# Column halves of w_out and 512-token MoE1 tiles in the first chunk of a windowed-attention and gated-MLP kernel

## The chip, the core and the metric

The kernel runs on one core of a Trainium2 chip. The metric is the time of one execution on the device in microseconds (us), lower is better. TensorE (PE) multiplies matrices into PSUM, which has eight banks of 128 partitions by 512 fp32 values here. ScalarE (ACT), VectorE (DVE), GpSimd (POOL) and SyncE (SP) are the other engines; POOL and SP here mainly issue DMAs.

## The reference

Attention over a causal window of 128 positions with a linear position bias, for 8 batches of 8 heads, 576 positions and head size 64; then a gated MLP on the 4608 resulting tokens of width 512.

```python
scores = scale * np.matmul(q, k.transpose(0, 1, 3, 2))
bias = slopes[:, None, None] * (-np.abs(rel).astype(np.float32))[None, :, :]
mask = (rel >= 0) & (rel < window)
scores = np.where(mask, scores + bias[None], -1000000000.0)
attn = np.exp(scores - np.max(scores, axis=-1, keepdims=True))
attn = attn / (np.sum(attn, axis=-1, keepdims=True) + 1e-09)
x = np.matmul(attn, v)          # (8, 8, 576, 64)
x = x.transpose(0, 2, 1, 3).reshape(4608, 512)
h = x @ w_in                    # w_in 512 x 2048
g = h * np.cos(h)
out = g @ w_out                 # w_out 2048 x 512
```

## The kernel before

**Stages.** The 4608 tokens are cut into nine chunks of 512. For each chunk, MoE1 computes h transposed: a feature block of 128 rows (fc, 16 of them) by tokens, summed over four blocks kc of the width 512. ScalarE takes sin(h + pi/2) from the PSUM bank into `cos`, VectorE multiplies bank and `cos` into the bf16 tile `gT`. MoE2 then computes, for each of the four 128-token tiles t of the chunk, 128 x 512 outputs as a sum of 16 matmuls over fc in one bank; ScalarE or VectorE copies the bank to `ob`, and SP stores it. MoE1 of later chunks (`moe1`) has matmuls of 512 tokens. MoE1 of chunk 0 (`moe1_block`) works by single tiles: a block is four features by 128 tokens in one bank, so it can start when one tile of x is there. There are 16 such blocks, in the hand-written list `order`, with banks in rotation from `seq`.

**Attention.** A unit (b, qb, hh) is one block of 128 queries of a batch and half of the heads, or all heads at the two ends (qb 0 and qb 4, the last of 64 queries). Its steps are scores on PE (`scores`), exp on ScalarE (`exps`), a multiplication by exp(bias) and mask on VectorE (`mask`), the product with v on PE (`pv`), a normalisation (`norm`), and a transpose into xT, on PE with a copy out of PSUM (`x_pe`) or by a DMA of SP (`x_dma`). Units in `BIASED` have the bias added on PE instead, as two matmuls of 512 columns with the identity ahead of their scores, and `mask` returns at once for them. Seven units of batch 0 come before chunk 0; the units for the next chunk's tokens are worked between MoE1 and MoE2 of each chunk. q and k of batches 0 and 1 are transposed on PE (`qk_transposes`, four banks and four copies for batch 1 and each of q and k); later batches' by DMAs of SP from `qnat` and `knat`.

**Banks.** `UB` = 2, 3 hold pv results, `OB` = 0, 1 the MoE2 results, `SB` = 4 to 7 scores; each is also used for other work.

**Order.** The class `Plan` takes all operations in the order in which the functions call `op`, with the buffers that each reads (`r`) and writes (`w`), an estimate of how long its engine is occupied (`occ`) and when its result is there (`lat`), and a priority `pri` (lower goes first). `schedule` lays out a fixed list for each engine from these estimates: among operations that are ready it takes the higher priority, then the earlier one. On the chip every engine runs its list in order and waits on semaphores. So a DMA that is really later than its estimate holds whatever stands behind its user in that engine's list. Attention has priorities 0 to 2, MoE1 3 to 5, MoE2 6, so that MoE2 fills the gaps of the attention. DMAs of POOL are issued in the order of the calls: `load_w_out` (line 429) issues four pieces, each of four feature blocks by all 512 columns, before `load_v(1)` and the loads of `qnat` and `knat`.

## Time and profile before

| | us |
|---|---|
| Median of three runs (309.72 to 310.37) | 310.05 |
| The profiled execution | 310.24 |
| Its span, first to last instruction | 308.4 |
| DVE busy | 195.8 |
| ACT busy | 200.3 |
| POOL busy | 97.0 |

The mean granted TensorE clock of the profiled execution was 1.000 of full speed. "Lnnn" is a line of the kernel; a row of a timeline has the start in us, the duration in us, the engine, the line, the operation, output and inputs, and how many instructions were merged; in square brackets stands the idle time of the engine before them and what ended it. Matmuls overlap: a merged row of n matmuls is longer than n times the issue interval by the length of the last one's pipeline, and some matmul records are missing, so the weight loads (PEld) count them better. The granted clock, the DMA share and GB/s stand at the end of the rows of a window.

### The profile page before, as it was taken

To read this page: it belongs to the slowest core of one execution; us is meant where nothing else is said; L and a number is where in the kernel's file an instruction comes from. 1 tells how busy PE (TensorE), PEld (TensorE's weight loads), DVE (VectorE), ACT (ScalarE), POOL (GpSimd) and SP (SyncE) were. 2 spreads that over 40 slices of the span, in tenths; PEclk is the share of its full clock that TensorE was granted. 3 is DMA by queue.
4 is the path that set the end of the run, shared out by engine and by line. 5 is a ranking of instruction groups with operands and counts; after the bars stand their busy time and mean duration, and the time that the engine had idled before them with its cause. 6 is when DMAs were issued, how large, how long until landed. Compare 5 with 4: busy or idle time off the path is not lost.

```text
span 308.4 us, 6675 instructions
## 1 busy us (share of the span) xinstructions
PE 299.5 (97%) x2685; PEld 162.1 (53%) x2726; DVE 195.8 (63%) x409; ACT 200.3 (65%) x267; POOL 97.0 (31%) x122
## 2 busy tenths in 40 slices
PE   8889999999999999999999999999999999999996
PEld 6679755445554455445544554455445554444444
DVE  7688777574668566856785568656966588742000
ACT  6887973875478745873688378746964488752211
POOL 8997200455055505550347123900500000000000
PEclk9999999999999999999999999999999999999999
DMA  9999999999499958998699969995991420001112
GB/s 147 179 204 207 206 162 193 132 183 154 122 121 138 172 98 154 133 175 98 157 114 149 167 88 180 150 184 114 143 113 44 113 70 0 0 0 70 68 71 99
DMA packets 150333, 39.09 MB, mean 127 GB/s; under 512 B 138912, under 2 KB 145312, under 8 KB 150304
## 3 DMA queue, kind: packets, MB, share of 16 engines
q0 software_dynamic: 100688, 18.10, 79.5%
q1 hardware_dynamic: 49344, 20.33, 33.3%
q8 instruction: 21, 0.34, 0.5%
q10 hardware_dynamic: 272, 0.26, 0.3%
q14 instruction: 8, 0.07, 0.1%
HBM read 36.70 MB, written 9.44 MB: 150 GB/s over the span
## 4 chain that ended last, share of the span: by engine, by line
PE 90%; DMA 3%; POOL 2%; ACT 2%; issue 1%; DVE 1%; POOLq 0%; ACTq 0%
PE ps L812 38%; PE ps L759 36%; PE ps L568 5%; PE ps L784 4%; DMA w_inb<-in_moe_w_in_dram 3%; ACT p L595 2%; PE ps L642 2%; PE ps L644 2%; PE ps L630 1%; POOL vp L391 1%; PE ps L509 1%; DVE p L614 1%; PE ps L634 1%; POOL qrows L383 0%; PE ps L721 0%
## 5 line engine op out<-in xcount | busy, mean ns | idle before, releaser
L812 PE MATMUL ps<-w_outb,gT 128*128 128x512 bf16 (+2 forms) x566 | 132.1, 373 | 2.5 <-issue 1.3
L759 PE MATMUL ps<-xT,w_inb 128*128 128x512 bf16 x499 | 113.9, 379 | 0.7
L768 DVE TENSOR_TENSOR gT<-ps,cos 128x512 bf16<-128x512 f32 x128 | 85.1, 688 | 19.6 <-ACT cos L764 14.7
L764 ACT ACTIVATE cos<-ps,halfpi 128x512 f32<-128x512 f32 x128 | 84.6, 687 | 18.0 <-PE ps L759 13.9
L812 PEld LDWEIGHTS ps<-w_outb,gT 128*128 128x128 bf16 x592 | 53.4, 98 | 55.7 <-DVE ob L820 0.3
L595 ACT ACTIVATE p<-ps 128x1024 bf16<-128x1024 f32 x64 | 61.5, 1023 | 31.2 <-PE ps L568 31.0
L759 PEld LDWEIGHTS ps<-xT,w_inb 128*128 128x128 bf16 x512 | 49.0, 98 | 56.2 <-ACT p L595 0.6
L391 POOL DMA_DIRECT2D vp<-in_v_dram x40 | 33.7, 870 | 87.6 <-DMA xT<-xnat 67.4
L614 DVE TENSOR_TENSOR p<-p,emask 128x1024 bf16<-128x1024 bf16 x59 | 39.7, 684 | 27.8 <-ACT p L595 27.8
L819 ACT ACTIVATE ob<-ps 128x512 f32<-128x512 f32 (+2 forms) x21 | 12.1, 576 | 41.6 <-PE ps L812 35.2
L402 POOL DMA_DIRECT2D qnat<-in_q_dram x30 | 25.3, 877 | 22.5 <-DMA qt<-qnat 22.5
L402 POOL DMA_DIRECT2D knat<-in_k_dram x30 | 25.4, 884 | 12.3 <-DMA kt<-knat 9.8
L820 DVE COPY ob<-ps 128x512 f32<-128x512 f32 x16 | 11.0, 685 | 15.8 <-PE ps L812 15.7
L681 DVE TENSOR_TENSOR xnat<-ps,rec 128x256 bf16<-128x256 f32 x48 | 19.9, 421 | 1.3
L568 PE MATMUL ps<-qt,kt 64*128 64x128 bf16 (+1 forms) x576 | 19.4, 211 | 0.3 <-DVE qt L525 0.2
L642 PEld LDWEIGHTS ps<-vp,p 128*128 128x128 bf16 x192 | 14.2, 97 | 9.9 <-issue 6.4
L568 PEld LDWEIGHTS ps<-qt,kt 64*128 64x128 bf16 x576 | 14.5, 94 | 8.7 <-issue 3.5
L642 PE MATMUL ps<-vp,p 128*128 128x65 bf16 x192 | 17.4, 193 | 0.7 <-DVE xT L731 0.5
L644 PE MATMUL ps<-vp,p 128*128 128x65 bf16 x192 | 17.5, 193 | 0.0
L784 PE MATMUL ps<-xT,w_inb 128*128 128x128 bf16 x256 | 16.0, 219 | 0.6 <-DMA w_inb<-in_moe_w_in_dram 0.6
L784 PEld LDWEIGHTS ps<-xT,w_inb 128*128 128x128 bf16 x256 | 14.5, 98 | 1.3 <-DMA w_inb<-in_moe_w_in_dram 0.8
L644 PEld LDWEIGHTS ps<-vp,p 128*128 128x128 bf16 x192 | 13.2, 97 | 2.2
(66 smaller groups left out, 160.9 us busy)
## 6 DMA issues: line engine op xcount, KB each, us to landing
out_dram<-ob SPq DMA_DIRECT2D x35, 256.0 KB, 2.2
vp<-in_v_dram POOLq DMA_DIRECT2D x32, 128.0 KB, 7.1
qnat<-in_q_dram POOLq DMA_DIRECT2D x24, 128.0 KB, 6.5
knat<-in_k_dram POOLq DMA_DIRECT2D x24, 128.0 KB, 5.1
w_outb<-in_moe_w_out_dram POOLq DMA_DIRECT2D x4, 512.0 KB, 21.8
w_inb<-in_moe_w_in_dram POOLq DMA_DIRECT2D x3, 512.0 KB, 12.2
qrows<-in_q_dram POOLq DMA_DIRECT2D x1, 576.0 KB, 15.5
krows<-in_k_dram POOLq DMA_DIRECT2D x1, 576.0 KB, 17.5
```

The lines of the kernel that those rows point to most:

```text
L391: op("pool", [lambda e, t=t, rows=rows: e.dma_start(vp[b % 2][0:rows, t, :, 0:64], v[b, :, 128 * t:128 * t + rows, :].rearrange("h p d -> ...
L402: fns.append(lambda e, t=t, rows=rows: e.dma_start(nat[which][0:rows, t, :, :], src[b, :, 128 * t:128 * t + rows, :].rearrange("h p d -> p ...
L568: ins = e.matmul(ps[:, banks[x], c0:c0 + n_], keys_ap(b, x, pr, kc), query_ap(b, x, pr, qb, n_), start=not acc, stop=stop)
L595: op("act", lambda e: e.activation(P[i][:, 0:1024], ps[:, banks[0]:banks[0] + 2, :].rearrange("p a b -> p (a b)"), ACTF.Exp, scale=0.125), ...
L614: op("dve", lambda e: e.tensor_tensor(p, p, m, ALU.mult), r=[("P", i), ("EM", 0), ("EM", 1)], w=[("P", i)], occ=600, lat=690, pri=1)
L642: e.matmul(o, P[i][:, c0:c0 + 128], V[:, qb - 1, h, 0:65], start=True, stop=False)
L644: ins = e.matmul(o, P[i][:, c0 + 128:c0 + 256], V[:, qb, h, 0:65], start=False, stop=True)
L759: op("pe", lambda e, kc=kc: e.matmul(ps[:, bank, :], w_in[:, kc, 128 * fc:128 * fc + 128], xT[:, kc, r0:r0 + CH], start=(kc == 0), stop=(k ...
L764: op("act", lambda e: e.activation(cosb[ci][:, :], ps[:, bank, :], ACTF.Sin, bias=halfpi[:, 0:1]), r=["halfpi"], w=[("B", bank), ("cos", c ...
L768: op("dve", lambda e: e.tensor_tensor(gT[gi][:, fc, :], ps[:, bank, :], cosb[ci][:, :], ALU.mult), r=[("cos", ci)], w=[("B", bank)] + [("g ...
L784: ins = e.matmul(ps[:, bank, 128 * i:128 * i + 128], w_in[:, kc, 128 * fc:128 * fc + 128], xT[:, kc, t0:t0 + 128], start=(kc == 0), stop=( ...
L812: op("pe", lambda e, t=t, fc=fc, bank=bank, j0=j0, j1=j1: e.matmul(ps[:, bank, 0:j1 - j0], gT[gi][:, fc, 128 * t:128 * t + 128], w_out[:, ...
```

## The change

Five things change, all in chunk 0 or ahead of it.

1. `BIASED` has one more unit, (0,3,0).
2. `load_w_out` loads w_out in quarters of eight feature blocks by 256 columns: columns 0-255 in pieces 0 and 1, columns 256-511 in pieces 2 and 3. The DMA's runs in DRAM become 1 KB instead of 2 KB, and 512 B instead of 1 KB in SBUF; the issue estimate goes from 750 to 900 ns.
3. `moe1_block` becomes `moe1_part`, which takes f1 - f0 features by t1 - t0 tiles with 512 values a partition in all: for features 0-3 single tiles as before, for features 4-7 two features by two tiles (matmuls of 256 columns), and features 8-15 go through `moe1` with 512-token matmuls. Banks come from a list.
4. The batch-1 transposes are called after the 11th and 14th of the sixteen and always use banks 2 to 5.
5. MoE2 of chunk 0 is `moe2_first`: for each half of the columns all four tiles in the order 0, 2, 1, 3, tiles 0 and 1 side by side in bank 0, tiles 2 and 3 in bank 1; a copy for each bank and a store of 256 rows by 256 columns.

```diff
@@ -336,7 +336,7 @@
         GROUPS = [[2] * 4] + [[3, 3, 2]] * 5 + [[3] * 3]
         SLOT = [4, 6, 2]
         QUOTA = [8, 8, 8, 8, 8, 8, 9]
-        BIASED = [(0, 0, 0)] + [(0, qb, hh) for qb in range(1, 3) for hh in range(2)]
+        BIASED = [(0, 0, 0)] + [(0, qb, hh) for qb in range(1, 4) for hh in range(2)][:5]
         SB, UB, OB = [4, 5, 6, 7], [2, 3], [0, 1]
 
         slopes = [2.0 ** (-8.0 * (h + 1) / H) for h in range(H)]
@@ -427,10 +427,13 @@
                lat=1300 * (f1 - f0))
 
         def load_w_out(u):
+
+            f0, j0 = 8 * (u % 2), 256 * (u // 2)
             op("pool", [lambda e: e.dma_start(
-                w_out[:, 4 * u:4 * u + 4, :],
-                moe_w_out[512 * u:512 * u + 512, :].rearrange("(f p) j -> p f j", p=128))],
-               w=[("wo", u)], dma=f"wo{u}", occ=750, lat=2600)
+                w_out[:, f0:f0 + 8, j0:j0 + 256],
+                moe_w_out[128 * f0:128 * f0 + 1024, j0:j0 + 256].rearrange(
+                    "(f p) j -> p f j", p=128))],
+               w=[("wo", u)], dma=f"wo{u}", occ=900, lat=2600)
 
         def constants():
             op("dve", lambda e: e.memset(zeros[:, :], 0.0), w=["zeros"], occ=60, pri=0)
@@ -770,32 +773,32 @@
                r=[("cos", ci)], w=[("B", bank)] + [("g", gi, fc, t) for t in range(4)], occ=606,
                lat=692, pri=3)
 
-        def moe1_block(t, f4, bank):
+        def moe1_part(f0, f1, t0, t1, bank):
 
             ci = ccount[0] % NCOS
             ccount[0] += 1
-            t0 = 128 * t
-            for i in range(4):
-                fc = 4 * f4 + i
-
-                def f(e, i=i, fc=fc):
+            n, w = f1 - f0, 128 * (t1 - t0)
+            for i in range(n):
+
+                def f(e, i=i):
                     ins = None
                     for kc in range(NPAIR):
                         ins = e.matmul(
-                            ps[:, bank, 128 * i:128 * i + 128],
-                            w_in[:, kc, 128 * fc:128 * fc + 128], xT[:, kc, t0:t0 + 128],
-                            start=(kc == 0), stop=(kc == NPAIR - 1))
+                            ps[:, bank, w * i:w * i + w],
+                            w_in[:, kc, 128 * (f0 + i):128 * (f0 + i) + 128],
+                            xT[:, kc, 128 * t0:128 * t1], start=(kc == 0), stop=(kc == NPAIR - 1))
                     return ins
-                op("pe", f, r=xkeys(range(NPAIR), t0, 128) + [("wi", fc // 2)], w=[("B", bank)],
-                   occ=232, lat=400, pri=5)
+                op("pe", f, r=xkeys(range(NPAIR), 128 * t0, w) + [("wi", (f0 + i) // 2)],
+                   w=[("B", bank)], occ=w * 427 // 256 + 18, lat=w * 427 // 256 + 186, pri=5)
             op("act", lambda e: e.activation(cosb[ci][:, :], ps[:, bank, :], ACTF.Sin,
                                              bias=halfpi[:, 0:1]),
                r=["halfpi"], w=[("B", bank), ("cos", ci)], occ=586, lat=687, table=1, pri=3)
             op("dve", lambda e: e.tensor_tensor(
-                gT[0][:, 4 * f4:4 * f4 + 4, t0:t0 + 128],
-                ps[:, bank, :].rearrange("p (i t) -> p i t", i=4),
-                cosb[ci][:, :].rearrange("p (i t) -> p i t", i=4), ALU.mult),
-               r=[("cos", ci)], w=[("B", bank)] + [("g", 0, 4 * f4 + i, t) for i in range(4)],
+                gT[0][:, f0:f1, 128 * t0:128 * t1],
+                ps[:, bank, :].rearrange("p (i t) -> p i t", i=n),
+                cosb[ci][:, :].rearrange("p (i t) -> p i t", i=n), ALU.mult),
+               r=[("cos", ci)],
+               w=[("B", bank)] + [("g", 0, fc, t) for fc in range(f0, f1) for t in range(t0, t1)],
                occ=606, lat=692, pri=3)
 
         def moe2(c):
@@ -812,7 +815,7 @@
                         op("pe", lambda e, t=t, fc=fc, bank=bank, j0=j0, j1=j1: e.matmul(
                             ps[:, bank, 0:j1 - j0], gT[gi][:, fc, 128 * t:128 * t + 128],
                             w_out[:, fc, j0:j1], start=(fc == 0), stop=(fc == NFC - 1)),
-                           r=[("g", gi, fc, t), ("wo", fc // 4)], w=[("B", bank)],
+                           r=[("g", gi, fc, t), ("wo", fc // 8), ("wo", 2 + fc // 8)], w=[("B", bank)],
                            occ=w * 427 // 1024 + 3, lat=w * 427 // 1024 + 166, pri=6)
                     o, i = ob[oi][:, 0:w], ps[:, bank, 0:w]
                     op(("act", "dve"),
@@ -824,6 +827,32 @@
                     op("sp", [lambda e, o=o, row=row, j0=j0, j1=j1: e.dma_start(
                         out[row:row + 128, j0:j1], o)],
                        r=[("ob", oi)], dma=f"st{oi}", occ=350, lat=0)
+
+        def moe2_first():
+
+            for y in range(2):
+                j0 = 256 * y
+                for t in (0, 2, 1, 3):
+                    for fc in range(NFC):
+                        op("pe", lambda e, t=t, fc=fc, j0=j0: e.matmul(
+                            ps[:, OB[t // 2], 256 * (t % 2):256 * (t % 2) + 256],
+                            gT[0][:, fc, 128 * t:128 * t + 128], w_out[:, fc, j0:j0 + 256],
+                            start=(fc == 0), stop=(fc == NFC - 1)),
+                           r=[("g", 0, fc, t), ("wo", 2 * y + fc // 8)], w=[("B", OB[t // 2])],
+                           occ=109, lat=275, pri=6)
+                for n, bank in enumerate(OB):
+                    oi = 2 * y + n
+                    o = ob[oi][:, :]
+                    i = ps[:, bank, :]
+                    op(("act", "dve"),
+                       {"act": lambda e, o=o, i=i: e.activation(o, i, ACTF.Copy),
+                        "dve": lambda e, o=o, i=i: e.tensor_copy(o, i)},
+                       w=[("B", bank), ("ob", oi)], occ={"act": 490, "dve": 606},
+                       lat={"act": 590, "dve": 691}, pri=6)
+                    o = out[256 * n:256 * n + 256, j0:j0 + 256].rearrange("(t p) j -> p t j", p=128)
+                    i = ob[oi][:, :].rearrange("p (t j) -> p t j", t=2)
+                    op("sp", [lambda e, o=o, i=i: e.dma_start(o, i)],
+                       r=[("ob", oi)], dma=f"st{oi}", occ=400, lat=0)
 
         ucount = [0]
 
@@ -910,17 +939,16 @@
         next_t, next_v = 2, 2
         for c in range(NCH):
             if c == 0:
-                seq = OB + SB[2:4] + SB[0:2]
-                order = [(0, 0), (1, 0), (2, 0), (0, 1), (1, 1), (2, 1), (3, 0), (3, 1)] + [
-                    (t, f4) for f4 in (2, 3) for t in range(4)]
-                at = 0
-                for i, (t, f4) in enumerate(order):
-                    moe1_block(t, f4, seq[at % 6])
-                    at += 1
-                    if i in (9, 12):
-                        qk_transposes(1, "q" if i == 9 else "k", 0, range(2),
-                                      UB + [seq[at % 6], seq[(at + 1) % 6]])
-                        at += 2
+                parts = [(0, 4, 0, 1), (0, 4, 1, 2), (0, 4, 2, 3), (4, 6, 0, 2), (6, 8, 0, 2),
+                         (0, 4, 3, 4), (4, 6, 2, 4), (6, 8, 2, 4)]
+                banks = [0, 1, 6, 7, 4, 5, 0, 1, 0, 1, 6, 7, 0, 1, 6, 7]
+                for i, bank in enumerate(banks):
+                    if i < len(parts):
+                        moe1_part(*parts[i], bank)
+                    else:
+                        moe1(0, i, bank)
+                    if i in (10, 13):
+                        qk_transposes(1, "q" if i == 10 else "k", 0, range(2), UB + SB[0:2])
                 load_nat("q", q, 2)
                 load_nat("k", k, 2)
             else:
@@ -941,7 +969,7 @@
                 if next_t < B:
                     load_nat("q", q, next_t)
                     load_nat("k", k, next_t)
-            moe2(c)
+            moe2_first() if c == 0 else moe2(c)
         R.schedule(filler=lambda e: e.matmul(ps[:, UB[1], 0:128], zeros[:, :],
                                              zeros[:, :], start=True, stop=True),
                    fill=(900, 8300))
```

## The prediction

> **What bounds the kernel now.** I read the page's busy times, the chain of work that ended last and the costliest groups, then the timelines of the engines around the edit, then the waits and windows of TensorE (PE) behind it.
>
> ```profile
> span 308.4 us, 6675 instructions
> PE 299.5 (97%) x2685; PEld 162.1 (53%) x2726; DVE 195.8 (63%) x409; ACT 200.3 (65%) x267; POOL 97.0 (31%) x122
> PE 90%; DMA 3%; POOL 2%; ACT 2%; issue 1%; DVE 1%; POOLq 0%; ACTq 0%
> L812 PE MATMUL ps<-w_outb,gT 128*128 128x512 bf16 (+2 forms) x566 | 132.1, 373 | 2.5 <-issue 1.3
> ```
>
> PE is busy for 97% of the span and is 90% of the chain. So a change gains only what it takes off PE's work or out of PE's waits, and loses only what it adds there. Most of a matmul's listed duration overlaps the next one; its price on PE is its share of a run of them, from the chain:
>
> ```profile
> 23.81 5.02 PE ps L784 x88
> 54.26 8.20 PE ps L759 x38
> ```
>
> The first row gives 57 ns for 128 columns (5.02/88), the second 216 ns for 512 (8.20/38). A line through both is 4 ns plus 0.414 ns a column, so I estimate 110 ns for 256 columns, a form of w_in and w_out matmul that the trace lacks.
>
> **The start, where PE still waits.** From PE's timeline:
>
> ```profile
> 17.33 0.84 PE L784 MATMUL ps<-xT,w_inb 128*128 128x128 bf16 x12 [0.63 <-DMA w_inb<-in_moe_w_in_dram]
> 18.01 0.19 PE L642 MATMUL ps<-vp,p 128*128 128x65 bf16 x1
> 19.47 0.20 PE L642 MATMUL ps<-vp,p 128*128 128x65 bf16 x1 [0.50 <-DVE xT L731]
> ```
>
> The brackets show 0.63 us until w_in's second piece lands, then 0.50 us until an eviction of x. The row at 18.01 is the pv of unit (0,3,0), the one at 19.47 that of (0,3,1). What goes before them, on ScalarE and VectorE:
>
> ```profile
> 16.74 1.02 ACT L595 ACTIVATE p<-ps 128x1024 bf16<-128x1024 f32 x1 [0.23 <-PE ps L568]
> ```
> ```profile
> 16.55 0.69 DVE L614 TENSOR_TENSOR p<-p,emask 128x1024 bf16<-128x1024 bf16 x1
> 18.55 0.66 DVE L614 TENSOR_TENSOR p<-p,emask 128x1024 bf16<-128x1024 bf16 x1
> 19.13 0.28 DVE L731 COPY xT<-ps 128x256 bf16<-128x256 bf16 x1
> ```
>
> Masks start at 16.55 and 18.55, for those two units. The second unit's exp ends at 17.76, yet its mask starts at 18.55 and the x eviction follows at 19.13. The edit of BIASED gives (0,3,0) its bias on PE: two matmuls of 512 columns (2 x 0.216 = 0.43 us) ahead of its scores. It takes away the first mask. The 0.43 us falls before 17.33, into the 0.63 us wait, and costs nothing there; if the list of PE leaves no room in that wait it costs 0.43. The pv of (0,3,0) no longer waits for a mask and may move into the wait too (0.25 us, from 18.01 to 18.26 by the next group; I take 0.2). VectorE, freed of 0.69 us, can evict x earlier, and most of the 0.50 us should go: I take 0.4. What is late next is w_in's third piece, which features 4-7 need. Together -0.6 us, bounds -1.1 (both waits gone) and +0.4 (none gone, bias paid).
>
> **MoE1 of chunk 0.** All 256 matmuls have 128 columns: 256 x 0.057 = 14.6 us. After: 64 of 128 columns, 32 of 256, 32 of 512: 64 x 0.057 + 32 x 0.110 + 32 x 0.216 = 14.1 us, so -0.5. With half of 216 or twice 57 for 256 columns it is -0.6 or -0.4. The cosines and products stay 16 of 128x512 each.
>
> **MoE2 of chunk 0.** 64 matmuls of 512 columns become 128 of 256: 64 x 0.216 = 13.8 against 128 x 0.110 = 14.1, so +0.3; bounds 0 (half of 216) and +0.8 (twice 57). Four evictions and four stores of 256 KB stay. A bank now holds two tiles; while it is emptied PE has the other bank's tile, 16 x 0.110 = 1.8 us, against the 0.69 us of the copy below. I cost this at nothing; if the copy queues behind two exps (1.94 us below) the cover is gone and up to 0.9 us is exposed, once.
>
> **The loads of w_out.** From POOL's timeline, the summary of these loads, and the load behind them:
>
> ```profile
> 15.07 3.00 POOL L430 DMA_DIRECT2D w_outb<-in_moe_w_out_dram  x4
> 18.02 4.24 POOL L391 DMA_DIRECT2D vp<-in_v_dram  x5
> DMA to landing us min/median/max: 19.1/21.8/24.6
> ```
> ```profile
> vp<-in_v_dram POOLq DMA_DIRECT2D x1, 128.0 KB, 24.8
> ```
>
> The pieces land between 34.2 (15.07 + 19.1) and 41.9 us (17.3 + 24.6), 2.57 us apart, and V of batch 1 at 42.8 (18.02 + 24.8). So transfer rate, not issue, sets these times. Half-column pieces have the same 512 KB in 1024 runs, twice as many and half as long. The nearest rows for such runs are w_in's first two pieces, 256 columns wide:
>
> ```profile
> 7.75 0.90 POOL L391 DMA_DIRECT2D vp<-in_v_dram  x1
> 8.61 2.27 POOL L423 DMA_DIRECT2D w_inb<-in_moe_w_in_dram  x3
> ```
> ```profile
> w_inb<-in_moe_w_in_dram POOLq DMA_DIRECT2D x1, 256.0 KB, 8.7
> vp<-in_v_dram POOLq DMA_DIRECT2D x1, 128.0 KB, 8.6
> ```
>
> The V tile lands at 16.35 (7.75 + 8.6), the 256 KB piece behind it at 17.3 (8.61 + 8.7): 0.96 us, less than half of 2.57. That bounds the extra cost below at 0. Above: a V tile is 1024 runs and lands 0.9 us behind the w_out piece before it (41.9 to 42.8), so 512 more runs cost at most 0.45 us a piece. I take 0.1, near the row of equal width; V of batch 1 then lands 0.4 us later, bounds 0 and 1.8. Issue on POOL may grow from 0.75 to V's 0.87 us, 0.5 us for four; the V and nat loads queued behind wait for the transfers anyway, so nothing.
>
> The Trainium skill, DMA: Bandwidth & Descriptors, section Why small descriptors are slow (HBM only), speaks against this part: a fixed overhead of about 3 cycles on each packet, one cycle for 32 bytes. By it a 512-byte run costs 38 cycles for what took 35, an estimate of +0.22 us a piece, where the row of w_in shows no such loss. By the page V would land 0.9 us later than now, not 0.4, and the sum below would come to -0.2 us if PE met all of that.
>
> **Around MoE2's start,** on PE, ScalarE and VectorE:
>
> ```profile
> 28.76 1.20 PE L509 MATMUL ps<-ident,qrows 128*64 128x128 bf16 x36
> 31.68 1.20 PE L509 MATMUL ps<-ident,krows 128*64 128x128 bf16 x36
> 35.68 0.63 PE L568 MATMUL ps<-qt,kt 64*128 64x64 bf16 x24
> 36.63 3.18 PE L812 MATMUL ps<-w_outb,gT 128*128 128x512 bf16 x14 [0.32 <-DVE gT L794]
> 43.62 0.42 PE L630 MATMUL ps<-vp,p 128*128 128x65 bf16 x8
> ```
> ```profile
> 35.78 0.69 ACT L791 ACTIVATE cos<-ps,halfpi 128x512 f32<-128x512 f32 x1 [0.23 <-PE ps L784]
> 36.48 1.28 ACT L595 ACT_TABLE_LOAD   x1
> 37.78 1.94 ACT L595 ACTIVATE p<-ps 128x1024 bf16<-128x1024 f32 x2
> ```
> ```profile
> 36.50 0.69 DVE L794 TENSOR_TENSOR gT<-ps,cos 128x512 bf16<-128x512 f32 x1 [0.22 <-ACT cos L791]
> 51.03 0.69 DVE L820 COPY ob<-ps 128x512 f32<-128x512 f32 x1 [0.38 <-PE ps L812]
> ```
>
> MoE2 starts at 36.63, right behind the scores of batch 0's tail. With 1.0 to 1.1 us saved it would start near 35.6. Then only the first two pieces are wanted, the second by 36.8 (34.2 + 2.57) or 0.2 later. Before it, two tiles of 8 matmuls, 16 x 0.110 = 1.8 us, are ready, so this wait is covered. The pv of (1,0,0) at 43.62 wants V at 42.8; moved up by 1 us it meets V at 43.2. PE's list can hold other MoE2 matmuls there; I take +0.1, bounds 0 and 0.6. The stores go through SP as before, 4 issues.
>
> **The sum** is -0.6 - 0.5 + 0.3 + 0.1 = -0.7 us at the start of chunk 1. Whether it lasts is decided at the next attention. PE's timeline there; the window of that stretch (length, then PE, PEld, VectorE, ScalarE and POOL busy, clock, DMA share, GB/s); SP's last key transpose and the landings of its kind; PE's waits from 60 to 120 us:
>
> ```profile
> 67.91 3.62 PE L812 MATMUL ps<-w_outb,gT 128*128 128x512 bf16 x16
> 71.46 0.85 PE L568 MATMUL ps<-qt,kt 64*128 64x64 bf16 x32
> 86.99 2.12 PE L759 MATMUL ps<-xT,w_inb 128*128 128x512 bf16 x8
> ```
> ```profile
> 67.91:86.99 19.08, 18.82 (x198) 9.95 (x200) 10.43 (x25) 9.75 (x13) 4.22 (x6) 1.00 1.11 131
> ```
> ```profile
> 63.68 1.25 SPq L414 DMA_TRANSPOSE kt<-knat  x1
> DMA to landing us min/median/max: 6.2/7.8/9.5
> ```
> ```profile
> PE ps L812 <- issue: 0.3, 2, 0.2
> ```
>
> The keys of batch 2 land at 69.9 (63.68 + 6.2); PE reaches their scores at 71.46. Between 67.91 and 86.99 PE is busy 18.82 of 19.08 us, and its waits from 60 to 120 come to 0.3 us: there it runs its list, which is fixed beforehand, without being held. So I expect the gain to be kept, as long as the list doesn't spend its MoE2 matmuls too early. The profiled run took 310.24 us, 1.84 around its span of 308.4; it stands 0.19 above the median 310.05. I put the change on the median: 310.05 - 0.7 = **309.3 us**, its own range 308.9 to 309.7.
>
> **The rivals.**
>
> *The chain of chunk 1 takes the gain back.* The w_out matmuls by stretch (their weight loads, PEld, have the full count):
>
> ```profile
> 36.30:54.10 17.80, 13.55 (x55) 5.12 (x59) 1.00 2.00 181
> 67.70:86.90 19.20, 15.89 (x65) 6.02 (x68) 1.00 1.12 131
> ```
>
> Of the 64 of chunk 0, 59 are done when chunk 1's MoE1 starts; the five open ones and 64 of the next make 69, and 68 of them are done when MoE1 of chunk 2 starts at 86.99. There is almost no filler left, so if the list puts the scores at 71.4 as now and fills the time before with more MoE2, PE arrives early and waits for the same exps, masks and evictions. Then only the last matmul (0.216) is gained: 309.8, range 309.6 to 310.3. For it: keys at 69.9 leave 1.5 us at most. Against: 0.3 us of waits now.
>
> *Slower: the new banks hold up the attention of chunk 0.* The scores at 35.68 need banks 4-7. Now the last MoE1 blocks are in 5, 0 and 1; after, features 14 and 15 are in 6 and 7, and both batch-1 transposes (28.76, 31.68) use 2 to 5, so the second waits for all four evictions of the first. The scores then come a cosine, a product and their hand-over (0.69 + 0.69 + 0.3 = 1.7 us) behind MoE1's end, not 0.3 behind it, and a second transpose that waits may add up to its own 1.2. That is 1.4 to 2.6 us later, less the 1.0 gained, so 0.4 to 1.6. The exps have some cover: they wait for the 1.28 us table load behind the last cosine anyway. It decides once this delay has used up the five open matmuls (5 x 0.216 = 1.1 us): from there PE is idle ahead of chunk 1, and its loss beyond 1.1 goes to the end. With the whole 2.6 us the loss is 2.6 - 1.1 = 1.5 against the 0.7 gained: 310.05 + 0.8 = 310.9, range 310.4 to 311.5. For it: banks 6 and 7 last. Against: PE's list may take 14 and 15 first, since it may choose among ready blocks.
>
> *More than the sum:* both waits of the start go (-1.1), and V costs nothing: -1.1 - 0.5 + 0.3 = -1.3, so 308.7, range 308.3 to 308.9.
>
> **How the numbers follow.** The sum 0.45, the chain that takes it back 0.24, the held attention 0.20, more than the sum 0.11. The range 308.5 to 310.9 leaves out about half of each outer case's far side. Differences under 0.2% (0.62 us) can't be told from none: faster means below 309.43, slower above 310.67. Faster: three quarters of the first (0.34), all of the last (0.11), a little of the second (0.02): 0.47. Slower: four fifths of the held case (0.16) and 0.02 of mishaps: 0.18. Same: 0.35.
>
> **What would show it.** In the start: no wait at 19.47, the scores now at 35.68 near 34.9, runs of 110 ns for 256 columns. V of batch 1 landing at 42.8 to 43.3. MoE1 of chunk 1 starting below 53.6. The gain kept: MoE1 of chunk 2 starting at 86.3 or below; taken back: new PE waits just before it. Wrong altogether: scores of chunk 0 behind 36.5, a wait of PE on w_out or V above 0.6, or the matmul of 256 columns at 114 ns or more.

## The result and the profile after

| | before | after |
|---|---|---|
| Median, us (22 runs each, on one chip) | 309.9 | 311.02 |
| Lowest to highest, us | 309.51 to 310.68 | 310.3 to 312.67 |
| The profiled execution, us | 310.24 | 311.86 |
| Its span, us | 308.4 | 309.7 |

The ratio after to before is 1.0033, 95% interval 1.0025 to 1.0040: about 1.0 us slower, where 0.7 us faster was forecast. The profiled execution of the changed kernel stands 0.84 us above its own median, so not every microsecond that it shows is there in every run. The medians decide below, the traces say where to look. One time of a later experiment (316.1 us in f1_short_rows) fell in a slow state of the chip and is left out of its row.

From the page of the changed kernel: span, busy times, chain of waits, and the group of the new MoE2 (busy us, mean ns of one, idle before).

```profile
span 309.7 us, 6547 instructions
PE 300.4 (97%) x2623; PEld 163.1 (53%) x2664; DVE 194.3 (63%) x407; ACT 200.9 (65%) x268; POOL 97.5 (31%) x122
PE 78%; DMA 11%; POOL 5%; ACT 3%; issue 1%; DVE 1%; POOLq 0%; ACTq 0%
L837 PE MATMUL ps<-w_outb,gT 128*128 128x256 bf16 x128 | 16.1, 273 | 0.0
```

PE's share of the chain fell from 90% to 78%, and DMA's rose from 3% to 11%. The 11% are two transfers, V of batch 1 (25.1 us from issue to landing) and the transpose of xfirst, the first block of batch 1, which MoE1 of chunk 1 needs (8.7 us). Such a share says where the chain passes, not what it costs: b1 below has 10% and loses 0.08%. The new MoE2 matmuls themselves have no idle time ahead of them.

PE's timeline of the changed kernel, at the start and around MoE2's start:

```profile
17.39 1.28 PE L786 MATMUL ps<-xT,w_inb 128*128 128x128 bf16 x20
19.31 1.04 PE L786 MATMUL ps<-xT,w_inb 128*128 128x128 bf16 x12
...
34.22 1.91 PE L837 MATMUL ps<-w_outb,gT 128*128 128x256 bf16 x16
36.20 0.63 PE L571 MATMUL ps<-qt,kt 64*128 64x64 bf16 x24
```

Both waits of the start (0.63 and 0.50 us) are gone, MoE1's last weight load stands at 33.78 instead of 35.38, and 16 MoE2 matmuls come ahead of the scores, which start 0.5 us later than before (36.20 against 35.68). The weight loads of those MoE2 matmuls stand 109 ns apart; the 16 take 34.22 to 36.13 with the last one's pipeline. The gain of 1.6 us up to here is more than the 1.1 of the sum: the start gave 1.1 instead of 0.6, as in the rival "More than the sum", and the tiles about 0.5.

What came next, in the table of PE's waits, then in that of its weight loads (total us, times, longest), then in PE's timeline:

```profile
PE ps L633 <- DMA vp<-in_v_dram: 0.8, 1, 0.8
PE ps L762 <- DMA xT<-xfirst: 0.6, 1, 0.6
PE ps L762 <- ACT p L598: 0.5, 1, 0.5
```
```profile
PEld ps L762 <- DMA xT<-xnat: 1.0, 1, 1.0
```
```profile
43.71 0.42 PE L633 MATMUL ps<-vp,p 128*128 128x65 bf16 x8 [0.82 <-DMA vp<-in_v_dram]
54.70 5.56 PE L762 MATMUL ps<-xT,w_inb 128*128 128x512 bf16 x25 [0.63 <-DMA xT<-xfirst]
121.37 0.82 PE L762 MATMUL ps<-xT,w_inb 128*128 128x512 bf16 x3 [0.47 <-ACT p L598]
```

There are three new waits between 36 and 125 us, where before had none over 0.3: on V of batch 1, on the transpose of xfirst that opens chunk 1's MoE1, and on an x transpose in chunk 3. The third is put down to ScalarE, but the weight loads ahead of those matmuls name the DMA. MoE1 of chunk 1 then starts at 54.47 instead of 54.03, that of chunk 2 at 87.66 instead of 86.99, and the last MoE2 matmul at 306.98 instead of 305.65.

Two views show what the DMAs do. First the queue totals (packets, MB, share of the 16 engines' span), before and then after:

```profile
q0 software_dynamic: 100688, 18.10, 79.5%
q1 hardware_dynamic: 49344, 20.33, 33.3%
```
```profile
q0 software_dynamic: 102736, 18.10, 82.7%
q1 hardware_dynamic: 49856, 20.33, 32.4%
```

The same bytes go in 2048 more packets on POOL's queue (w_out, whose runs are half as long) and in 512 more on SP's (the stores of chunk 0, whose rows of 256 fp32 are half as long too). The second number was nowhere in the prediction. Then SP's own list around chunk 0's stores, before and after, and each time the transfer of xfirst (us from issue to landing):

```profile
41.48 1.28 SPq L743 DMA_TRANSPOSE xT<-xtail  x1
45.37 0.36 SPq L824 DMA_DIRECT2D out_dram<-ob  x1
45.78 1.24 SPq L743 DMA_TRANSPOSE xT<-xfirst  x1
47.07 0.64 SPq L824 DMA_DIRECT2D out_dram<-ob  x1
50.30 5.47 SPq L411 DMA_TRANSPOSE qt<-qnat  x1
```
```profile
xT<-xfirst SPq DMA_TRANSPOSE x1, 7.1
```
```profile
41.86 1.27 SPq L746 DMA_TRANSPOSE xT<-xtail  x1
43.19 2.41 SPq L854 DMA_DIRECT2D out_dram<-ob  x2
45.75 1.38 SPq L746 DMA_TRANSPOSE xT<-xfirst  x1
54.69 4.02 SPq L411 DMA_TRANSPOSE qt<-qnat  x1
```
```profile
xT<-xfirst SPq DMA_TRANSPOSE x1, 8.7
```

The first two banks are finished earlier, so both stores now go ahead of xfirst, where before one went ahead and one behind. xfirst is issued at the same time and lands at 54.4 instead of 52.9. The q transposes of batch 2 are issued 4.4 us later, since the last piece of `qnat`, queued behind w_out and V on POOL, lands at 54.67 instead of 50.28.

### The profile page after: what moved, and what is told of

The parts are those of the page before. It is cut to its first block, busy times and chain, and to the rows that moved or that the text cites. A ratio compares the mean times of both kernels' runs of the same rounds, so it can differ in the third digit from the quotient of the medians.

```text
span 309.7 us, 6547 instructions
## 1 busy us (share of the span) xinstructions
PE 300.4 (97%) x2623; PEld 163.1 (53%) x2664; DVE 194.3 (63%) x407; ACT 200.9 (65%) x268; POOL 97.5 (31%) x122
## 4 chain that ended last, share of the span: by engine, by line
PE 78%; DMA 11%; POOL 5%; ACT 3%; issue 1%; DVE 1%; POOLq 0%; ACTq 0%
PE ps L762 35%; PE ps L815 33%; DMA vp<-in_v_dram 8%; PE ps L571 4%; DMA xT<-xfirst 3%; ACT p L598 3%; PE ps L645 1%; PE ps L647 1%; POOL vp L391 1%; PE ps L633 1%; POOL w_inb L423 1%; POOL w_outb L432 1%; POOL qrows L383 1%; POOL krows L383 1%; DVE p L617 1%
## 5 line engine op out<-in xcount | busy, mean ns | idle before, releaser
L762 PE MATMUL ps<-xT,w_inb 128*128 128x512 bf16 x527 | 120.8, 379 | 2.0 <-DMA xT<-xfirst 0.6
L815 PE MATMUL ps<-w_outb,gT 128*128 128x512 bf16 (+2 forms) x506 | 116.9, 372 | 1.9 <-issue 1.1
L771 DVE TENSOR_TENSOR gT<-ps,cos 128x512 bf16<-128x512 f32 x136 | 90.5, 688 | 21.1 <-ACT cos L767 16.2
L767 ACT ACTIVATE cos<-ps,halfpi 128x512 f32<-128x512 f32 x136 | 90.1, 687 | 19.9 <-PE ps L762 14.8
L762 PEld LDWEIGHTS ps<-xT,w_inb 128*128 128x128 bf16 x544 | 51.8, 98 | 60.7 <-DMA xT<-xnat 1.0
L815 PEld LDWEIGHTS ps<-w_outb,gT 128*128 128x128 bf16 x528 | 47.8, 98 | 50.2
L645 PEld LDWEIGHTS ps<-vp,p 128*128 128x128 bf16 x192 | 14.1, 97 | 8.6 <-issue 5.6
L823 DVE COPY ob<-ps 128x512 f32<-128x512 f32 x13 | 9.0, 689 | 15.4 <-PE ps L815 15.2
L837 PE MATMUL ps<-w_outb,gT 128*128 128x256 bf16 x128 | 16.1, 273 | 0.0
L837 PEld LDWEIGHTS ps<-w_outb,gT 128*128 128x128 bf16 x128 | 11.8, 98 | 1.9
```

The lines of the kernel that those rows point to most:

```text
L645: e.matmul(o, P[i][:, c0:c0 + 128], V[:, qb - 1, h, 0:65], start=True, stop=False)
L762: op("pe", lambda e, kc=kc: e.matmul(ps[:, bank, :], w_in[:, kc, 128 * fc:128 * fc + 128], xT[:, kc, r0:r0 + CH], start=(kc == 0), stop=(k ...
L767: op("act", lambda e: e.activation(cosb[ci][:, :], ps[:, bank, :], ACTF.Sin, bias=halfpi[:, 0:1]), r=["halfpi"], w=[("B", bank), ("cos", c ...
L771: op("dve", lambda e: e.tensor_tensor(gT[gi][:, fc, :], ps[:, bank, :], cosb[ci][:, :], ALU.mult), r=[("cos", ci)], w=[("B", bank)] + [("g ...
L815: op("pe", lambda e, t=t, fc=fc, bank=bank, j0=j0, j1=j1: e.matmul(ps[:, bank, 0:j1 - j0], gT[gi][:, fc, 128 * t:128 * t + 128], w_out[:, ...
L837: op("pe", lambda e, t=t, fc=fc, j0=j0: e.matmul(ps[:, OB[t // 2], 256 * (t % 2):256 * (t % 2) + 256], gT[0][:, fc, 128 * t:128 * t + 128] ...
```

## The experiments

Each label is one kernel, timed 7 to 12 times. Ratios are to the kernel before, timed on the same chip beside it; "after" is 1.0033 [1.0025, 1.0040]. A ratio is not the quotient of two medians, from which it differs by up to 0.12% (for c4 that quotient is 1.0054, for d3 0.9999). Different rows come in part from different chips, so they are compared by their ratios. Times like "MoE1 of chunk 1 at" are PE's weight loads in that kernel's own profiled execution. Executions differ in such times by half a us and more: MoE1's first matmul stood between 14.1 and 15.1 in all but one of them.

| kernel | what it is | median, us | ratio [95%] |
|---|---|---|---|
| c4_halves_only | before + halves of w_out and MoE2 | 311.80 | 1.0042 [1.0024, 1.0059] |
| d1_no_halves | after without them | 309.93 | 0.9997 [0.9988, 1.0006] |
| c3_moe1_only | before + new MoE1 of chunk 0 | 309.70 | 0.9983 [0.9970, 0.9997] |
| c2_biased_only | before + new BIASED | 310.24 | 1.0006 [0.9992, 1.0020] |
| c1_old_biased | after with the old BIASED | 310.58 | 1.0022 [1.0004, 1.0039] |
| b1_runs | before + w_out in 512-byte runs | 310.45 | 1.0008 [0.9998, 1.0018] |
| a1_store_behind | after, two stores behind xfirst | 311.24 | 1.0042 [1.0026, 1.0058] |
| a2_v_ahead | after, V ahead of the last w_out piece | 310.64 | 1.0018 [1.0003, 1.0033] |
| a3_both | a1 and a2 together | 310.93 | 1.0023 [1.0009, 1.0038] |
| d2_x2_ahead | after, a store behind chunk 3's x transpose | 310.97 | 1.0035 [1.0021, 1.0049] |
| d4_told | after, planner told two landings | 310.67 | 1.0024 [1.0014, 1.0035] |
| e1_no_x2 | a3, third store behind the keys | 310.48 | 1.0007 [0.9993, 1.0021] |
| d3_all_stores | e1 and d2 together | 310.08 | 1.0006 [0.9992, 1.0020] |
| e3_act_stores | after, three stores issued by ScalarE | 310.58 | 1.0006 [0.9994, 1.0018] |
| f1_short_rows | c3, chunk 0's stores in rows of 1 KB | 310.25 | 1.0001 [0.9984, 1.0018] |
| f2_whole_rows | after, chunk 0's stores in whole rows | 310.62 | 1.0019 [1.0008, 1.0030] |

### Which part of the change costs

c4 has only the new `load_w_out`, `moe2_first` and its call; d1 is the changed kernel with those three undone:

```diff
 c4_halves_only, against before (d1_no_halves, against after, the other way round)
-                w_out[:, 4 * u:4 * u + 4, :],
+                w_out[:, f0:f0 + 8, j0:j0 + 256],
...
-                           r=[("g", gi, fc, t), ("wo", fc // 4)], w=[("B", bank)],
+                           r=[("g", gi, fc, t), ("wo", fc // 8), ("wo", 2 + fc // 8)], w=[("B", bank)],
...
-            moe2(c)
+            moe2_first() if c == 0 else moe2(c)
```

> The kernel before with only the column halves of w_out and MoE2 of chunk 0 by halves; MoE1 and BIASED as before. Theory W: V lands 0.5 to 0.9 later than 42.8 and PE asks for it at 43.6, a wait of 0 to 0.3; the two stores stand ahead of xfirst's transpose, which lands near 54.4, so MoE1 of chunk 1 starts 0.3 to 0.6 later; 0.2 to 0.3 us more matmul: ratio 1.0015 to 1.0035, most of the loss of the whole change. Theory B or H: ratio 0.9995 to 1.001.

> The changed kernel with w_out's loads and MoE2 of chunk 0 as before: what stays is the new MoE1 and the new BIASED. Theory (the loss sits in the halves alone, and the MoE1 part brings 0.5 to 1 us): ratio to before 0.997 to 0.9995, MoE1 of chunk 1 at 53.0 to 53.9, its successor at 85.5 to 86.3, last MoE2 at 304.3 to 305.2. Rival (the new BIASED and the new MoE1 together upset the list as well): ratio 1.001 or more.

c4 costs 0.42% and d1 nothing, so the loss sits in the halves. c4's ratio is above its theory's 1.0035; only one store stood ahead of its xfirst, not two, and V, which landed at 42.98, was not waited for. c4's waits between 36 and 125 us (total us, times, longest) are on the same transposes as in the changed kernel, though its MoE1 and BIASED are the old ones:

```profile
PE ps L762 <- DMA xT<-xfirst: 0.5, 1, 0.5
...
PE ps L762 <- DMA xT<-xnat: 0.2, 1, 0.2
```

d1 shows none of them: it has no row but one of 0.3 us for issue. Its MoE1 of chunk 1 (53.28) and of chunk 2 (85.81) start inside the expected windows, 0.8 and 1.2 us earlier than before's, yet its median ratio is 0.9997, above the upper edge of "0.997 to 0.9995". Its profiled execution, 309.37 us, is the fastest of its twelve; that one flatters it by 0.56 us. And d1 has the scores of chunk 0's end 2.4 us behind the end of MoE1, as the changed kernel has, because banks 6 and 7 hold MoE1's last results. PE has MoE2 matmuls in between. No loss is seen from it: c3 below has the scores 2.6 us behind and is faster than before.

c3 and c2 are the other two parts alone, and c1 the whole change without its BIASED:

```diff
 c2_biased_only, against before (c1_old_biased, against after, the other way round)
-        BIASED = [(0, 0, 0)] + [(0, qb, hh) for qb in range(1, 3) for hh in range(2)]
+        BIASED = [(0, 0, 0)] + [(0, qb, hh) for qb in range(1, 4) for hh in range(2)][:5]
 c3_moe1_only, against before: moe1_part, parts and banks of the change
-                    moe1_block(t, f4, seq[at % 6])
+                    if i < len(parts):
+                        moe1_part(*parts[i], bank)
+                    else:
+                        moe1(0, i, bank)
```

> The kernel before with only the new MoE1 of chunk 0 (parts of two tiles, 512-token matmuls, listed banks); w_out and MoE2 as before. PE has 0.5 us less to do. Theory W: no late DMA, MoE1 of chunk 0 ends 0.5 to 1.0 earlier, scores near 36 because of banks 6 and 7, chunk 1 keeps 0 to 0.5: ratio 0.9985 to 1.000. Theory H (scores held by banks 6 and 7 are the loss, by 0.5 to 1.0 us): ratio 1.0015 to 1.003.

> The kernel before with only the new BIASED list. Theory W: w_out's runs and the stores are as before, so V lands at 42.8 and xfirst's transpose near 52.9; PE saves about 0.5 us in the start and chunk 1 keeps 0 to 0.5 of it: ratio 0.9985 to 1.000. Theory B: two more matmuls of 512 columns are paid, ratio 1.0015 or above. Theory K (any earlier arrival of PE is taken back by the attention of chunk 1, which starts with the keys of batch 2): MoE1 of chunk 1 starts 0.3 to 0.5 earlier than 54.0, MoE1 of chunk 2 at 86.8 to 87.0 all the same, ratio 0.999 to 1.001.

> The changed kernel with the old BIASED list (unit (0,3,0) masked on VectorE again); the lists of all engines are laid out anew. Theory W (the loss is made by two late DMAs, V of batch 1 behind the finer w_out runs and the transpose of xfirst behind two stores; a faster start is eaten by them): the start loses about 0.5 us but the waits on V and xfirst shrink by as much, so the time stays at a ratio of 1.002 to 1.004. Theory B (the bias on PE is the loss): ratio 1.000 or below.

The MoE1 part alone is 0.17% faster than before, 0.53 us (interval 0.1 to 0.9), and beats both kernels; its MoE1 of chunk 1 starts with no wait, and chunk 2's at 85.91. Its MoE1 of chunk 0 ends 1.35 us earlier, counted from the first matmul, since the wait for w_in went too. BIASED alone takes away the wait for w_in, as this row, gone in c2, had it in before, and moves the end of chunk 0's MoE1 up by 0.7 us counted from its first matmul:

```profile
PE ps L784 <- DMA w_inb<-in_moe_w_in_dram: 0.6, 1, 0.6
```

But the ratio of c2 is 1.0006, its interval holds 1, and c1 is no slower than the changed kernel without it. So nothing of that gain can be measured at the end. Why isn't settled: c2's ratio is the one of its theory K, but its MoE1 of chunk 2 starts 0.56 us earlier than before's, not at the same time as K said; and c2's profiled run has 0.5 us of new waits on `gT` ahead of the scores, one execution's evidence. The two parts also overlap: the wait for w_in is gone with the new MoE1 alone (c3, c1) as well, and beside it the new BIASED removes only the 0.5 us wait for the x eviction.

### What of the halves costs: the loads in shorter runs

b1 keeps before's pieces and lists, each piece in two DMAs of 256 columns, so with runs half as long, as in the change:

```diff
-            op("pool", [lambda e: e.dma_start(
+            op("pool", [lambda e, j=j: e.dma_start(
-                w_out[:, 4 * u:4 * u + 4, :],
-                moe_w_out[512 * u:512 * u + 512, :].rearrange("(f p) j -> p f j", p=128))],
+                w_out[:, 4 * u:4 * u + 4, j:j + 256],
+                moe_w_out[512 * u:512 * u + 512, j:j + 256].rearrange("(f p) j -> p f j", p=128))
+                for j in (0, 256)],
```

> The kernel before, lists unchanged, with each of its four w_out pieces loaded as two column halves, so that w_out has 4096 runs of 512 B instead of 2048 of 1 KB and nothing else differs. If the shorter runs are what makes V late: the last piece lands 0.5 to 0.9 us later than 41.9 and the first V tile at 43.3 to 43.7 instead of 42.8; PE asks for V at 43.6, so the time rises by 0.1 at most, 309.9 to 310.1. If the shorter runs cost nothing and V is late for another reason (issue on GpSimd, transposes beside it): V at 42.8 to 43.0.

The short runs and the four DMAs more cost 0.08%, 0.25 us, with 1 still in the interval. The theory's landings came: the last piece at 42.70 and V at 43.63 instead of 42.79, with the load ahead of w_out landing as before (31.70, 31.72). So all of w_out took 0.87 us longer, 0.22 for each quarter, here in eight DMAs. In the change's four DMAs a piece takes about 0.1 us more: in the changed kernel the first three land at 33.70, 36.36 and 39.01, 2.65 us apart, where before's stood 2.54 apart. The changed kernel's own loads, from POOL's timeline, and their summary:

```profile
15.06 3.52 POOL L432 DMA_DIRECT2D w_outb<-in_moe_w_out_dram  x4
```
```profile
DMA to landing us min/median/max: 18.6/21.3/25.0
```

The last piece (17.7 + 25.0 = 42.7) came 3.7 us behind the third, and V 0.95 behind it. That 3.7 isn't in every trace: where the last of such pieces still stands ahead of V, it is 3.61 in c1, 4.18 in e3 and 3.79 in f2, but 2.66 to 2.85 in a1, c4, d2 and d4. With the pieces of before (before, c2, c3, d1, f1) it is 2.50 to 2.76. Whether the new pieces bring this stall isn't shown: each kernel has one trace. So V, 0.9 us later than in before (43.66 against 42.79), is made of 0.4 us of longer pieces and 1.0 us of a stall that four of these eight traces have, less 0.6 us by which the loads ahead of w_out ended earlier (31.11 against 31.72).

### Moving transfers within the changed kernel's lists

After the lists are laid out, single operations are moved in them. Nothing else is changed.

```diff
         R.schedule(...)
+        def behind(what, mark):      # move what(o) right behind mark(o)
+            ...
 a1, a3, d3, e1 (xf: the transpose of xfirst of batch 1)
+        behind(lambda o: o.dma in ("st0", "st1") and o.start < xf.start, lambda o: o is xf)
 a2, a3, d3, e1 (v1: V tile 1 of batch 1)
+        behind(lambda o: o.dma == "wo3", lambda o: o is v1)
 d3, e1 (kt: key transposes of batch 2)
+        behind(lambda o: o.dma == "st2" and o.start < kt.start, lambda o: o is kt)
 d2, d3 (st: the store right ahead of chunk 3's last x transpose x2)
+        behind(lambda o: o is st, lambda o: o is x2)
```

> The changed kernel with its own fixed lists; only on SyncE's list the two stores of the first column half now stand behind the DMA transpose of xfirst instead of ahead of it. Theory S (two stores in SP's queue ahead of that transpose make it land late and hold MoE1 of chunk 1): the transpose lands near 52.9 us as before the change, not 54.4, the 0.63 us wait at the start of MoE1 of chunk 1 is gone and the time falls by 0.6, to about 310.4 (ratio to before 1.0015). Theory V (only the late V of batch 1 costs, by 0.8 to 1.0 us): no change, 311.0, ratio 1.0033. Theory L (the new lists of the later chunks are simply worse): no change.

> The changed kernel with its own fixed lists; only on GpSimd's list the last piece of w_out is issued behind the first two V tiles of batch 1 instead of ahead of them. The first V tile then lands near 40 us instead of 43.7. Theory V: the 0.8 us wait at 43.7 is gone and the time falls by 0.8 to 1.0, to about 310.1 (ratio 1.0005). Theory S (the transpose of xfirst is bound by its place behind the stores): the wait at 43.7 goes, but MoE1 of chunk 1 still starts near 54.5 and its wait grows from 0.6 to about 1.4 us; the time stays at 310.8 to 311.0. If the last piece of w_out becomes late, a new wait of PE on it stands near 47.

> Both moves at once, lists otherwise those of the changed kernel. Theories S and V together: both waits go, MoE1 of chunk 1 starts at 53.0 to 53.6 and the time is 309.4 to 309.8 (ratio 0.998 to 1.000). If the lists of the later chunks cost by themselves, or if chunk 1 takes the gain back, it stays above 310.2.

Each repair did its own job in the trace. With the stores behind it, xfirst landed at 52.39 in a1, 7.0 us from its issue as in before, and MoE1 of chunk 1 started without a wait, at 53.48 in a1 and 52.99 in a3. With V ahead, it landed at 41.6 and its wait was gone. But the time of a1 didn't fall. The largest wait of a1, and then of a3, in that stretch (total us, times, longest):

```profile
PE ps L571 <- DMA kt<-knat: 1.2, 1, 1.2
```
```profile
PE ps L571 <- DMA kt<-knat: 0.5, 1, 0.5
```

PE arrived at the scores of chunk 1 earlier and waited there for the keys of batch 2, which landed at 72.69 and 71.44, where the changed kernel had them at 69.35 and before at 69.87. So in these traces the gain was given back 18 us later. a2's 1.0018 lies above the 1.0005 of its theory V, and xfirst's wait didn't grow as theory S said. a3's 1.0023 isn't told apart from a2's 1.0018.

> The changed kernel, and in SP's list one store of chunk 2's results (issued at about 116.5) goes behind the x transpose that stands after it, the one that MoE1 of chunk 3 waits 0.85 us for at 120.3. Theory (the transpose is late because its data queue behind the store's): it lands before 119.6, the wait is below 0.2, everything from there on 0.6 to 0.9 earlier, last MoE2 at 306.1 to 306.4, ratio 1.0005 to 1.0025. Rival (PE has one MoE2 matmul less to fill with there, and some other wait comes in its place): last MoE2 within 0.3 of 306.98, ratio 1.003 or more.

In d2's SP list the transpose now goes first:

```profile
115.92 1.17 SPq L749 DMA_TRANSPOSE xT<-xnat  x1
117.14 0.58 SPq L827 DMA_DIRECT2D out_dram<-ob  x1
```

It landed at 119.70, 3.8 us from its issue instead of 4.4, and the wait at 120 is gone: the profile matched the theory. The time didn't: 310.97 and 1.0035, as the rival had it. The profiled execution, 310.32, was the lowest of its seven. So moving that store doesn't win back the loss.

> All the repairs of order at once: chunk 0's first two stores behind the transpose of xfirst, its third store behind the key transposes of batch 2, the last w_out piece behind V tiles 0 and 1, and the store of the run before behind the x transpose of chunk 3. Theory (the loss is made of late transfers behind stores and loads): MoE1 of chunk 1 at 52.8 to 53.3, keys of batch 2 at 70.3 or earlier, MoE1 of chunk 2 at 86.2 or earlier, no wait over 0.2 at 120, last MoE2 at 304.3 to 305.0, ratio 0.9975 to 0.9995. Rival (the keys are set by the load queue on POOL, which the halves have made later): keys at 71 or later, scores of chunk 1 right behind them, last MoE2 at 305.2 or later, ratio 1.000 to 1.003.

> The kernel with all repairs of order, but the store in chunk 2's run stays ahead of the x transpose of chunk 3. So beside the two repairs that gave 1.0023 before, only chunk 0's third store behind the key transposes is new. Theory (that store, ahead of the keys, was the one that took the gain back): ratio 0.9995 to 1.0015, scores of chunk 1 not held by the keys, a wait of 0.4 to 0.7 at 120. Rival (the store before the x transpose is worth the most): ratio 1.002 or more.

With the third store also behind the key transposes, the ratio falls to 1.0007 in e1 and 1.0006 in d3: most of the loss is gone, with no change to what is computed or loaded. d3's rival gave 1.000 to 1.003, and that is where it came out, but not for the rival's reason: the keys landed at 70.03, as the theory had it, and MoE1 of chunk 2 still started at 86.93 instead of 86.2. By the ratio, no run of repairs got below before. The one DMA wait of d3 between 36 and 125 us:

```profile
PE ps L762 <- DMA xT<-xnat: 0.3, 1, 0.3
```

That is the wait of chunk 3, although the store stands behind the transpose; e1, where the store stays ahead, has none. d3 and e1 differ by this store and by nothing in time, which agrees with d2. e1's interval overlaps a3's, so the share of the third store by itself isn't settled. In e1's profiled execution the keys were late again, although the third store stood behind them; their transposes were issued at 61.06, when the last piece of `knat` had landed:

```profile
PE ps L571 <- DMA kt<-knat: 0.7, 1, 0.7
```

> The changed kernel with chunk 0's first three stores issued by ScalarE, on its own queue, at the same places in time; SP's list has only the transposes there. Theory (a transpose waits for the store ahead of it in the same queue): xfirst lands at 53.2 or earlier, no wait on it, as when the stores were put behind it; ratio 1.000 to 1.0025, since V stays late. Rival (the transfers share the same engines whichever queue they come from): xfirst lands at 54 or later and PE waits for it as now; ratio 1.003 or more.

```diff
+        for o in R.order:
+            if o.dma in ("st0", "st1", "st2") and o.start < kt.start:
+                o.eng = ("act",)
```

The ratio is 1.0006, as low as with all the moves, though V is where the change put it. But the landing isn't what theory said. SP's list of e3, ScalarE's issues, and the transfer of xfirst (us from issue to landing):

```profile
46.78 1.29 SPq L746 DMA_TRANSPOSE xT<-xfirst  x1
55.46 3.88 SPq L411 DMA_TRANSPOSE qt<-qnat  x1
```
```profile
44.33 0.44 ACTq L854 DMA_DIRECT2D out_dram<-ob  x1
46.26 0.38 ACTq L854 DMA_DIRECT2D out_dram<-ob  x1
```
```profile
xT<-xfirst SPq DMA_TRANSPOSE x1, 8.4
```

xfirst still takes 8.4 us, on a queue with no store ahead of it. So its place in SP's queue isn't what stretches it. The Trainium skill, DMA: Bandwidth & Descriptors, section Queues, rings and completion order, says that each DMA engine takes the queues that have work in turn, packet by packet. The 8.4 us agree in so far as a queue of its own didn't spare the transpose the stores. PE didn't wait for it here because this execution's MoE1 began 1.9 us later (first matmul at 16.34, against 14.46) and the loads only 0.7 to 1.0 us later. e3's theory gave the ratio right and the landing wrong, its rival the landing right and the ratio wrong. That the three stores in SP's list cost 0.27% is shown (the intervals 1.0025 to 1.0040 and 0.9994 to 1.0018 don't meet); how they cost it, when xfirst is as slow without them there, isn't settled. What e3 also changes is that the later transposes of q and k no longer stand behind the third store.

### The form of the stores

Laid beside each other, the kernels sort by the form of what is stored ahead of xfirst. With one or two stores of 256 columns issued in the 3 us before it, it took 8.0 to 8.7 us (after, a2, c1, c4, d2, d4, e3); with stores of whole rows ahead, even two of them in c3, or with none, it took 6.6 to 7.2 (before, b1, c2, c3, d1, a1, a3, d3, e1). f1 gives the short rows to c3, f2 takes them from the changed kernel; all else stays. c3's list and its transfer first:

```profile
43.74 1.13 SPq L824 DMA_DIRECT2D out_dram<-ob  x2
45.47 1.31 SPq L743 DMA_TRANSPOSE xT<-xfirst  x1
```
```profile
xT<-xfirst SPq DMA_TRANSPOSE x1, 7.0
```

```diff
 f1_short_rows, against c3_moe1_only
-                    op("sp", [lambda e, o=o, row=row, j0=j0, j1=j1: e.dma_start(
-                        out[row:row + 128, j0:j1], o)],
+                    cut = [(j0, j1)] if c else [(0, 256), (256, 512)]
+                    op("sp", [lambda e, oi=oi, row=row, j0=j0, a=a, b=b: e.dma_start(
+                        out[row:row + 128, a:b], ob[oi][:, a - j0:b - j0]) for a, b in cut],
 f2_whole_rows, against after: in moe2_first, for each half y, bank n and its tile s
+                    oi = 2 * n + s
+                    o, i = ob[oi][:, j0:j0 + 256], ps[:, bank, 256 * s:256 * s + 256]
...
+                    if y:
+                        op("sp", [lambda e, oi=oi: e.dma_start(
+                            out[128 * oi:128 * oi + 128, :], ob[oi][:, :])],
```

> The fastest kernel so far (before with the new MoE1 of chunk 0, 0.9983), with each of chunk 0's stores cut into two of 256 columns, so that they have the halves' 1 KB rows; places in SP's list, w_out and MoE2 are those of that kernel. Theory (the stores of the halves hurt by their short rows, that is by their packets: with two whole-row stores ahead of it xfirst took 7.0 us, with two of short rows 8.4 to 8.7): xfirst takes 8.0 us or more from issue to landing, ratio 0.9995 to 1.002, that is 0.1 to 0.35% over that kernel. Rival (their place and time in the list, not their form): xfirst takes 6.6 to 7.4 us, ratio 0.997 to 0.9992.

> The changed kernel with MoE2 of chunk 0 still by halves, but each tile's two halves copied into one buffer of 512 columns and stored once, in whole rows, after the second half: twice the copies at half the width, and no store ahead of xfirst. Theory (the early stores in short rows carry most of the loss): xfirst lands within 7.4 us of its issue, PE waits for it less than 0.2, ratio 1.000 to 1.0015. Rival (half-width MoE2 or the later w_out carry it): ratio 1.0025 or more.

From f1: SP's list, the transfer of xfirst, and PE's waits between 36 and 125 us:

```profile
45.18 2.17 SPq L825 DMA_DIRECT2D out_dram<-ob  x4
47.40 1.26 SPq L743 DMA_TRANSPOSE xT<-xfirst  x1
```
```profile
xT<-xfirst SPq DMA_TRANSPOSE x1, 8.6
```
```profile
PE ps L759 <- DMA xT<-xfirst: 1.3, 1, 1.3
...
PE ps L812 <- DMA w_outb<-in_moe_w_out_dram: 0.5, 1, 0.5
```

Short rows, in twice as many DMAs, took the transpose from 7.0 to 8.6 us, and PE waits 1.3 us for it where c3 had no such wait. That wait isn't made by the rows alone: xfirst landed 3.5 us later than in c3, 1.6 of it in transit and 1.9 by its issue, which four issues in place of two and a start 1.4 us later held up. With the transit of c3 it would have landed at 54.4, before PE asked for it at 54.7 (an estimate from these rows). The ratio rose by 0.18%, from 0.9983 to 1.0001, as theory had it, but the intervals overlap. f1's eleven times fall into two groups, 309.35 to 310.25 and 310.9 to 311.5, as if the wait were met in some executions and not in others; that isn't shown. From f2, the same transfer and PE's wait that is left:

```profile
xT<-xfirst SPq DMA_TRANSPOSE x1, 7.4
```
```profile
PE ps L633 <- DMA vp<-in_v_dram: 0.7, 1, 0.7
```

The wait on xfirst is gone, and 1.0033 becomes 1.0019, between theory's 1.0015 and the rival's 1.0025. So by the middle values the short, early stores are one part of the loss, 0.14% here and 0.18% in f1, and not the whole; V, late behind w_out, remains. f2's interval overlaps that of the changed kernel, and f2 changes two things, the rows and the time of the stores, of which c3 with its two early stores of whole rows speaks for the rows.

### What the planner believes

```diff
-               w=[("wo", u)], dma=f"wo{u}", occ=900, lat=2600)
+               w=[("wo", u)], dma=f"wo{u}", occ=900, lat=3500 if u == 3 else 2600)
...
-                    occ=1250, lat=500)
+                    occ=1250, lat=2500 if b == 1 and qb == 0 else 500)
```

> The changed kernel, with the planner told two landings as measured: the last w_out piece 0.9 us later (and so what is queued behind it on POOL), and the transpose of xfirst of batch 1 2 us later. Nothing else is edited; all lists are laid out anew. Theory (the lists spend MoE2 matmuls too early because they believe in landings that don't come): the waits on V and xfirst are below 0.2 each, and about 1 us comes back: last MoE2 at 305.8 to 306.3, ratio 1.000 to 1.0015. Rival (the landings themselves bind, and PE has no work to put into the gaps): waits vanish there but scores or MoE1 of chunks 1 to 3 start as late as in the changed kernel, last MoE2 306.7 or later, ratio 1.0025 or more.

The waits on V and xfirst vanished from the profile (no row of either is left), 64 MoE2 matmuls were spent when chunk 1's MoE1 began instead of 59.5, and the last MoE2 matmul came at 305.46. But the ratio is 1.0024 [1.0014, 1.0035], at the edge of the rival's, though the late scores and the last MoE2 matmul at 306.7 that the rival named did not come. In this execution V also landed at 42.70, without the stall, so its wait isn't gone by the estimates alone, and it is 0.46 us faster than d4's median. About a quarter of the loss lies there, if any: the intervals overlap.

## Why the prediction was wrong

**The start, -0.6: more in the trace, nothing in the time.** Both waits went, 1.1 us, the outer bound. But the 0.63 us for w_in also go with the new MoE1 alone, so the two terms share them. c2, the same edit alone, is not faster (1.0006), so the step "-0.6 us" was sized where PE stood at 36 us, and what PE gained there it didn't keep.

**MoE1 of chunk 0, -0.5: right.** The issue interval of 256 columns is 109 ns against the estimate of 110. c3's 0.53 us agrees, partly by luck, since it also holds what is left of the wait for w_in.

**MoE2's matmuls, +0.3, and the hand-over of banks, 0: right as far as seen.** 128 x 0.109 = 14.0 us, and no idle time in front of them.

**The loads of w_out: right in the rate, short of the wait.** A piece took 0.1 us more, as taken (0.22 in b1's eight DMAs). V was forecast at 0.4 us later and came 0.9 later in the profiled run, with the stall of the last piece; the wait of PE was 0.82 us against "+0.1, bounds 0 and 0.6". The shorter runs, measured by b1, are worth 0.25 us, in an interval that holds zero. By the rule of the Trainium skill, DMA: Bandwidth & Descriptors, section Why small descriptors are slow (HBM only), a piece would have cost 0.22 us more, an estimate; the 0.1 measured in the change's pieces is half of that.

**The step that failed** is "The stores go through SP as before, 4 issues", which was counted at nothing. They don't go as before: both stand ahead of xfirst, 2 us earlier, and in rows half as long, while the transposes of xfirst and of batch 2's q and k are in flight. The earlier time comes with the new MoE1 too (c3's stores are issued at 43.74 and 44.54) and did no harm there; the short rows come with the halves. xfirst then takes 8.0 to 8.7 us where it took 7, and has 1.1 us to spare. Whole rows, stored behind xfirst, brought the ratio from 1.0033 to 1.0019 (f2); issuing the three stores from ScalarE, or behind the transposes with V put ahead, to 1.0006 (e3, e1, d3). So their size is 0.14 to 0.27%, 0.4 to 0.8 us. That the wait for xfirst is how they cost it is not shown: a1 took that wait away and stayed at 1.0042, e3 kept the slow transfer and lost next to nothing. With those, 0.25 us for the runs, -0.53 for MoE1, 0.2 for c2 and 0.2 for MoE2's matmuls, the sum is 0.5 to 0.9 us against 1.0 measured; each term from a ratio has an interval of about 0.4 us on either side, so the agreement is weak evidence.

**"So I expect the gain to be kept"** was drawn from PE's 0.3 us of waits in chunks 1 to 3 of before. That row says that PE wasn't held there, not how much later a transfer may come before it holds PE. The keys of batch 2 landed 1.6 us ahead of their use, xfirst 1.1 ahead of MoE1. A change that brings PE forward by 0.7 and xfirst back by 1.5 has spent that margin, and the traces of a1 and a3 show the keys' margin spent as soon as the first is repaired.

**The rivals.** The slower one had the right sign with the wrong mechanism: the scores of chunk 0 did come 0.5 us later because of banks 6 and 7, the low end of its 0.4 to 1.6, but d1 and c3 have the same delay and lose nothing. Of the signs named for "wrong altogether", the one that came true was the wait on V above 0.6. "The chain of chunk 1 takes the gain back" described a1 and a3, PE early and waiting for the keys, not the changed kernel itself.
